# Forgetting attention and an FFN on one core: q and k loaded once for a pair of heads, and one values matmul for the high and low parts of the last 64 by 64 block

## The chip, the core and the metric

The kernel runs on one core of a Trainium2 chip. The core has TensorE for matmuls (PE in the profile; its weight loads, which overlap with the matmuls, have a row of their own, PEld), VectorE (DVE), ScalarE (ACT), GpSimd (POOL) and SyncE (SP), whose queue issues all DMAs of this kernel. They run side by side and wait for one another through semaphores. The metric is the device time of one execution in microseconds, lower is better.

## What is computed

For 8 batches of 8 heads, 576 positions and 64 features a head, causal attention with a decay that is the difference of running sums of log f; the result, 4608 tokens by 512 features, goes through a two-layer FFN with a leaky ReLU.

```python
scores = scale * np.matmul(q, k.transpose(0, 1, 3, 2))
cum = np.cumsum(np.log(np.clip(f, 0.0001, 1.0)), axis=-1)
decay = cum[:, :, :, None] - cum[:, :, None, :]
scores = np.where(causal, -1000000000.0, scores + decay)
scores = scores - np.max(scores, axis=-1, keepdims=True)
attn = np.exp(scores)
attn = attn / (np.sum(attn, axis=-1, keepdims=True) + 1e-09)
x = np.matmul(attn, v)            # heads side by side: (4608, 512)
h = x @ w_in                      # (4608, 2048)
out = np.maximum(0.01 * h, h) @ w_out
```

## The kernel before

All products are made from operands that are rounded to a shorter format (fp32r) for one pass through TensorE. So each operand is kept as a high part and a low part (the rest), and a product is two or three matmuls: high by high, high by low, low by high.

**The FFN** is cut into 18 groups of 256 tokens. `ffn()` yields after each small piece of work (a quantum: 12 matmuls into `h`, or 6 into the sums `o`), and `fill(step)` puts so many quanta between the steps of the attention, so that TensorE always has something to do. Between the layers ACT makes `g`, DVE its rounded part `gh` (L551), and GpSimd the rest `gl` (L553).

**The attention** treats the first 256 positions of three batches ahead of the rest (`early_...`). Then comes one task for each of the 64 heads: `t` 0 to 7 are batch 0, positions 256 to 575; 8 to 47 are five batches with all positions; 48 to 63 are the last two batches, positions from 256 on again. The main loop works on two heads at once: in loop `t`, `scores(t, i)` makes five blocks of rows of head `t`, `transposes(t - 1, i)` and `values(t - 1)` finish head `t - 1`, `load(t + 1)` stands at the top of the loop, and `split(t + 1)` near its end.

- `load` (L223) brings q and k of one head twice, into the lower and the upper 64 partitions of `qraw` and `kraw` (64 features are only half of the partitions); for an even head also v of a pair (`fixed_vm`, L227 and L228).
- `split` (L337 to L347): ACT rounds q to `s1` and k to `m1` on all 128 partitions; a DMA copies the upper half of `s1` to `fixed_s2` (L339); two small DMAs bring decay rows (L340, L341); GpSimd takes the differences into `s1` and `fixed_m2` (L133, the helper `minus`); ACT and GpSimd make the high and low half of the columns of `fixed_vs`, the weights of the values matmuls.
- `scores` (L362 to L376): two matmuls a block, `m1` by `s1` and `m2` by `s2`; DVE adds the mask `tri` and takes the row extreme (L367); ACT takes the exponential (L373) and leaves the block in `fixed_z0` to `fixed_z4`. Block `z4` is 128 rows by 576 columns; its last 64 columns belong to the ragged end of the sequence, and the 64 columns behind them are zero from the start.
- `transposes` (L412): the blocks go through TensorE into a PSUM buffer named `tr`; ACT copies the rounded part to `ph` (L424), DVE the rest to `pl` (L426). `tr_t_1`, the step with i = 1, takes the lower half of the diagonal blocks, and in it the end of `z4`.
- `values` (L451): for each of 4 to 5 column blocks one matmul from `ph` and one from `pl`, all into one PSUM buffer `av` with the weights `fixed_vs`. For the last block, of 64 columns, both have only 64 of 128 partitions that are not zero. ACT and DVE add the two halves of the result to `x` (L458, L459), which frees the buffer.
- `inverse` (L469 to L482) after each second head: the reciprocal sums go to DRAM and come back spread over partitions as `rb` and `rbr`; `normalise` multiplies `x` with them and writes it out, and `xs<-xd` later loads it as an FFN group.

`av`, `tr` and `rt` (of `inverse`) share two PSUM buffers that take turns: each use waits until the one before the last has been read out. Each engine runs its instructions in the order of its list. That order comes from a scheduler with times of its own, not only from the order of the code.

Of the kernel before, what the change touches and what calls it, by code (L numbers as in the profile page):

```python
# [8 lines left out]
F32 = mybir.dt.float32  # L9
# [4 lines left out]
ALU = mybir.AluOpType  # L14

P = 128
# [21 lines left out]
def forgetting_attention_ffn(ctx, tc, qT, kT, v4, vr, f, w_in, w_out, out):  # L38
# [175 lines left out]

    def load(t):

        s, c0, c1 = tasks[t]
        h = state[t] = {}
        a, n = c0 * P, S
        for name, src, lo in (("q", qT, a), ("k", kT, 0)):  # L220
            x = h[name] = one.tile([P, S], F32, tag=f"{name}raw", name=f"{name}raw_{t}")
            for o in range(2):
                nc.sync.dma_start(x[o * D:(o + 1) * D, lo:n], src[s][:, lo:n])  # L223
        if s % 2 == 0:
            g = s // 2
            vm = fixed["vm"]
            nc.sync.dma_start(vm[:, :, :NFULL], v4[g])  # L227
            nc.sync.dma_start(vm[:REST, :, NFULL], vr[g])  # L228
            pairs[s // 2, c0] = {}
# [97 lines left out]
    def split(t):  # L327
# [4 lines left out]
        a, n = c0 * P, S  # L332
        x = "ab"[t % 2]
        s1 = h["s1"] = one.tile([P, S], F32R, tag="s1", name=f"s1_{t}", bufs=2)
        m1 = h["m1"] = one.tile([P, S], F32R, tag="m1", name=f"m1_{t}", bufs=2)
        s2, m2 = h["s2"], h["m2"] = fixed["s2" + x], fixed["m2" + x]
        nc.scalar.copy(s1[:, a:n], h["q"][:, a:n])  # L337
        nc.scalar.copy(m1[:, :n], h["k"][:, :n])
        nc.sync.dma_start(s2[D:, a:n].bitcast(F32), s1[D:, a:n].bitcast(F32))  # L339
        nc.sync.dma_start(s2[2:4, a:n].bitcast(F32), dec_q[s][:, a:n])  # L340
        nc.sync.dma_start(m2[:2, :n].bitcast(F32), dec_k[s][:, :n])  # L341
        minus(s1[:D, a:n], h["q"][:D, a:n], s1[:D, a:n].bitcast(F32))
        minus(m2[D:, :n], h["k"][D:, :n], m1[D:, :n].bitcast(F32))
        o = s % 2
        vs, vm = fixed["vs"][:, o], fixed["vm"][:, o]
        nc.scalar.copy(vs[:, :, :D], vm)
        minus(vs[:, :, D:], vm, vs[:, :, :D].bitcast(F32))  # L347

    def scores(t, i):
# [9 lines left out]
        for x, (a, b) in enumerate(parts):  # L359
# [6 lines left out]
            at = TRI - P + m - n + a  # L366
# [9 lines left out]
        )  # L376

# [10 lines left out]
    def transposes(t, i):  # L388
# [6 lines left out]
        todo, runs, at = [], [], pieces(t, i)[0][3]  # L395
        for x, j, q, skip, m in pieces(t, i):
            todo.append((at - skip, x, j))
            to = place_p(j, q)
            last = runs[-1] if runs else None
            if last and last[4] == 1 and last[1] + last[2] == to:  # L400
                last[2] += m
            elif last and last[2] == m and last[4] > 1 and last[4] * last[3] + last[1] == to:
                last[4] += 1
            elif last and last[2] == m and last[4] == 1 and to > last[1]:
                last[3], last[4] = to - last[1], 2
            else:
                runs.append([at, to, m, 0, 1])
            at += m
# [6 lines left out]
        for dst, eng in ((h["ph"], "a"), (h["pl"], "v")):  # L415
            for a, to, m, step, n in runs:
                if n == 1:
                    o, hi, src = dst[:, to:to + m], h["ph"][:, to:to + m], ps[:, a:a + m]
                else:
                    o = strided(dst, to, n, step, m)  # L420
                    hi = strided(h["ph"], to, n, step, m)
                    src = ps[:, a:a + n * m].rearrange("p (j m) -> p j m", m=m)
                if eng == "a":
                    nc.scalar.copy(o, src)  # L424
                else:
                    nc.vector.tensor_tensor(o, src, hi.bitcast(F32), op=ALU.subtract)  # L426

    def strided(t, start, n, step, m):
        a = t[:, start:start + m]
        return bass.AP(tensor=a.tensor, offset=a.offset, ap=[a.ap[0], [step, n], [1, m]])  # L430
# [208 lines left out]
    for t in range(nt + 1):  # L639
        heads[0] = t < nt  # L640
        if t + 1 < nt:
            load(t + 1)
# [61 lines left out]
```

## Time and profile before

| | |
|---|---|
| three runs | 1220.94 to 1221.28 us, median 1221.16 |
| the profiled execution | 1219.51 us, its span 1217.7 us |
| granted TensorE clock | 0.947 |
| busy: PE, ACT, DVE, POOL | 1193.7, 631.0, 612.8, 429.3 us |
| DMA | 110.54 MB, mean 91 GB/s |
| instructions | 22171 |

The busy time of PE counts each matmul until its last result is out, and matmuls overlap, so it says that PE was seldom empty, not that it ran at its best. What a matmul really takes up is read from the distances between weight loads. In a row of a timeline stand the start in us, the duration in us, engine, line, operation, output<-inputs, the shape (partitions x elements) and in brackets the idle time ahead of it and what ended it. In a row of groups stand the count, the busy sum in us and the mean in ns.

### The profile page before, as it was taken

What the parts mean: (1) busy time and instruction counts of PE and PEld (TensorE: products, weight loads), DVE (VectorE), ACT (ScalarE), POOL (GpSimd) and SP (SyncE); (2) the same over time, 40 slices, a digit from 0 to 9 for tenths busy, and PEclk for the clock granted to TensorE, in tenths of its full rate; (3) what the DMA queues carried; (4) which work ended last, traced back from release to release, by engine and by line L of the source; (5) the groups of instructions that cost most, each with busy time, mean ns of one, the idle gap of its engine ahead of it and who ended that gap; (6) DMA issues with size and microseconds to landing.
All of it is one profiled execution on the core that took longest, in us unless ns stands there. A gap on an engine that the chain in (4) does not pass through costs nothing.

```text
span 1217.7 us, 22171 instructions
## 1 busy us (share of the span) xinstructions
PE 1193.7 (98%) x7876; PEld 1077.6 (88%) x7876; DVE 612.8 (50%) x1682; ACT 631.0 (52%) x1631; POOL 429.3 (35%) x347
## 2 busy tenths in 40 slices
PE   8899999989999999999999999999999999999998
PEld 6678899988889999999999999999999998999997
DVE  7889556656645455544554434344444334553111
ACT  6876456667755565555544545455444444552111
POOL 1000354445444344444434434343344334432000
PEclk9899999989999999999999999999999999999999
DMA  6555234344342233323322223231223122211000
GB/s 208 167 193 171 81 96 119 89 133 112 100 125 80 81 97 107 97 71 96 97 89 60 89 69 95 74 94 54 79 75 92 58 75 75 75 54 46 18 18 19
DMA packets 81103, 110.54 MB, mean 91 GB/s; under 512 B 19616, under 2 KB 50704, under 8 KB 80992
## 3 DMA queue, kind: packets, MB, share of 16 engines
q1 hardware_dynamic: 80992, 109.11, 29.7%
q8 instruction: 63, 1.03, 0.4%
q14 instruction: 48, 0.39, 0.1%
HBM read 82.62 MB, written 18.58 MB: 83 GB/s over the span
## 4 chain that ended last, share of the span: by engine, by line
PE 86%; DMA 5%; DVE 4%; ACT 3%; issue 1%; POOL 0%; SPq 0%; ACTq 0%; DVEq 0%; POOLq 0%
PE h L541 31%; PE o L574 31%; PE av L451 8%; PE tr L412 7%; PE sc L362 7%; DMA xs<-xd 2%; DMA xd<-x 1%; PE sce L256 1%; DVE fixed_z L367 1%; DMA qraw<-in_qT 1%; PE ave L298 1%; DVE pl L426 1%; ACT fixed_z L373 0%; DMA wraw<-in_w_out 0%; DMA wraw<-in_w_in 0%
## 5 line engine op out<-in xcount | busy, mean ns | idle before, releaser
L541 PE MATMUL h<-xh,win_h 128*128 128x256 f32 x1152 | 331.3, 288 | 0.3 <-ACT xh L306 0.3
L541 PE MATMUL h<-xh,win_l 128*128 128x256 f32 x1152 | 327.6, 284 | 0.0
L541 PE MATMUL h<-xs,win_h 128*128 128x256 f32 x1024 | 289.3, 282 | 0.0
L553 POOL TENSOR_TENSOR gl<-g,gh 128x512 fp32r<-128x512 f32 x111 | 143.3, 1291 | 323.9 <-DVE gh L551 315.5
L574 PE MATMUL o<-wout_h,gh 128*128 128x512 f32 x576 | 233.2, 405 | 0.0
L574 PE MATMUL o<-wout_l,gh 128*128 128x512 f32 x576 | 227.0, 394 | 0.0
L574 PE MATMUL o<-wout_h,gl 128*128 128x512 f32 x576 | 225.6, 393 | 0.0
L541 PEld LDWEIGHTS h<-xh,win_h 128*128 128x128 f32 x1152 | 219.9, 191 | 3.5 <-ACT xh L306 0.8
L541 PEld LDWEIGHTS h<-xh,win_l 128*128 128x128 f32 x1152 | 220.3, 191 | 0.8 <-issue 0.7
L373 ACT ACTIVATE fixed_z<-fixed_z,max 128x192 f32<-128x192 f32 (+3 forms) x272 | 161.0, 592 | 105.1 <-DVE max L367 101.2
L367 DVE CUSTOM_DVE_ANT_0 fixed_z<-sc,tri 128x192 f32<-128x192 f32 (+3 forms) x272 | 121.8, 450 | 164.9 <-PE sc L362 162.9
L424 ACT CAST ph<-tr 128x64 fp32r<-128x64 f32 (+3 forms) x360 | 127.0, 374 | 147.2 <-PE tr L412 108.3
L548 ACT ACTIVATE g<-h 128x512 f32<-128x512 f32 x144 | 85.9, 597 | 217.4 <-PE h L541 214.7
L541 PEld LDWEIGHTS h<-xs,win_h 128*128 128x128 f32 x1024 | 195.3, 191 | 2.1
L426 DVE TENSOR_TENSOR pl<-tr,ph 128x64 fp32r<-128x64 f32 (+3 forms) x360 | 145.8, 422 | 76.2 <-ACT ph L424 75.3
L551 DVE CAST gh<-g 128x512 fp32r<-128x512 f32 x144 | 69.0, 479 | 193.9 <-ACT g L548 191.0
L412 PE MATMUL tr<-ident_r,fixed_z 128*128 128x128 f32 x888 | 146.8, 276 | 4.9 <-DVE x L459 2.7
L133 POOL TENSOR_TENSOR s<-qraw,s 64x576 fp32r<-64x576 f32 (+1 forms) x64 | 78.6, 1229 | 190.0 <-ACT s L337 185.3
L412 PEld LDWEIGHTS tr<-ident_r,fixed_z 128*128 128x128 f32 x888 | 109.0, 140 | 24.8 <-DVE x L459 2.9
L574 PEld LDWEIGHTS o<-wout_h,gl 128*128 128x128 f32 x576 | 108.4, 188 | 24.1 <-DVE maxe L269 0.4
L362 PE MATMUL sc<-m,s 128*128 128x288 f32 (+1 forms) x336 | 121.1, 365 | 3.6 <-DVE max L367 3.5
L574 PEld LDWEIGHTS o<-wout_h,gh 128*128 128x128 f32 x576 | 109.0, 189 | 15.7 <-issue 0.4
(107 smaller groups left out, 1687.6 us busy)
## 6 DMA issues: line engine op xcount, KB each, us to landing
kraw<-in_kT SPq DMA_DIRECT2D x128, 144.0 KB
qraw<-in_qT SPq DMA_DIRECT2D x80, 144.0 KB
wraw<-in_w_in SPq DMA_DIRECT2D x16, 512.0 KB
wraw<-in_w_out SPq DMA_DIRECT2D x16, 512.0 KB
fixed_vm<-in_v SPq DMA_DIRECT2D x32, 256.0 KB
xs<-xd SPq DMA_DIRECT2D x16, 512.0 KB
out<-ost SPq DMA_DIRECT2D x28, 256.0 KB
xd<-x SPq DMA_DIRECT2D x20, 288.0 KB
```

Of the source, the lines that this page charges most:

```text
L133: nc.gpsimd.tensor_tensor(out, a, b, op=ALU.subtract)
L362: nc.tensor.matmul(ps[:, :b - a], h["s" + w][:, q:q + P], h["m" + w][:, a:b], start=y == 0, stop=y == 1,)
L367: nc.vector.tensor_tensor_reduce(out=z[:, a:b], in0=ps[:m, :b - a], in1=tri[:m, at:at + b - a], scale=-SCALE, scalar=3.0e38 if x == 0 else ...
L373: nc.scalar.activation(z, z, AF.Exp, bias=h["max"][:m, last:last + 1], scale=-1.0, accum_out=fixed["sum" + "ab"[s // 2 % 2]][:m, i, s % 2: ...
L412: nc.tensor.transpose(ps[:, a:a + P], fixed[f"z{x}"][:, j * P:(j + 1) * P], ident)
L424: nc.scalar.copy(o, src)
L426: nc.vector.tensor_tensor(o, src, hi.bitcast(F32), op=ALU.subtract)
L451: nc.tensor.matmul(ps[:, a - lo:hi - lo], fixed["vs"][:, odd, j, :], h[w][:, at:at + hi - a], start=(n == 0), stop=(n == len(steps) - 1),)
L541: nc.tensor.matmul(ph[:, e, :], w[:, c, fs], xx[:, c, :], start=(c == 0 and x == 0), stop=(c == NCC - 1 and x == 2),)
L548: nc.scalar.activation(g, ph, AF.Prelu, alpha=0.01)
L553: eng.tensor_tensor(gl, g, gh.bitcast(F32), op=ALU.subtract)
L574: nc.tensor.matmul(acc[k], gg[:, e, ts], w[:, e, :], start=(fc_ == 2 * p0 and x == 0), stop=(fc_ == 2 * p1 - 1 and x == 2),)
```

## The change

Three things are changed.

**One load for a pair of heads.** `load` runs only ahead of an even head, at the third step of the loop instead of its top, and puts q and k of the even head into the lower, of the odd head into the upper partitions. What needs a head on the other half is made by copies that move it across partitions: ACT writes one half and DVE, with two new casts a head, the other. The DMA from `s1` to `fixed_s2` is gone. The decay rows keep their own place at the top of the loop (`load_decay`).

**One matmul for the last block.** GpSimd copies the last 64 columns of `z4` into the 64 columns behind them, so that its transpose has the block on both halves of the partitions. ACT's high part is then on both halves, DVE subtracts it in place on the upper half, and GpSimd copies the weights of the block to the upper half as well. One matmul with 128 partitions so adds high and low; the one from `pl` is left out.

**Smaller things.** The mask tile is 128 columns shorter, `rb` and `rbr` are one tile (two DMAs for four), and the row that goes to DRAM lies in a tile with the tag `y`, which `values` uses too.

```diff
     def load(t):
+        for name, src, lo in (("q", qT, a), ("k", kT, 0)):
+            x = raw[name] = one.tile([P, S], F32, tag=f"{name}raw", name=f"{name}raw_{t}")
+            nc.sync.dma_start(x[:, lo:], src[s:s + 2, :, lo:].rearrange("s d n -> (s d) n"))
...
+    def load_decay(t):
...
+        s2, m2 = h["s2"], h["m2"] = fixed["s2" + x], fixed["m2" + x]
+        nc.sync.dma_start(s2[2:4, a:].bitcast(F32), dec_q[s][:, a:])
+        nc.sync.dma_start(m2[:2].bitcast(F32), dec_k[s])
...
     def split(t):
-        nc.scalar.copy(s1[:, a:n], h["q"][:, a:n])
-        nc.scalar.copy(m1[:, :n], h["k"][:, :n])
-        nc.sync.dma_start(s2[D:, a:n].bitcast(F32), s1[D:, a:n].bitcast(F32))
...
-        minus(s1[:D, a:n], h["q"][:D, a:n], s1[:D, a:n].bitcast(F32))
-        minus(m2[D:, :n], h["k"][D:, :n], m1[D:, :n].bitcast(F32))
...
+        mine, other = (low, up) if o == 0 else (up, low)
+        k, q = raw["k"][mine], raw["q"][mine, a:]
+        near, far = (s1[low, a:], s2[up, a:]) if o == 0 else (s2[up, a:], s1[low, a:])
+        nc.scalar.copy(m1[mine], k)
+        nc.vector.tensor_copy(m1[other], k)
+        nc.scalar.copy(near, q)
+        nc.vector.tensor_copy(far, q)
+        minus(m2[up], k, m1[mine].bitcast(F32))
+        minus(s1[up, a:], q, near.bitcast(F32))
...
+        nc.gpsimd.tensor_copy(vs[REST:, NFULL], vs[:REST, NFULL].bitcast(F32))
     def scores(t, i):
...
+        if i == NFULL:
+            z = fixed[f"z{i}"][m - REST:]
+            nc.gpsimd.tensor_copy(z[:, n:], z[:, n - REST:n])
     def transposes(t, i):
...
+        for a, to, m in twice:
+            x = ph[REST:, to:to + m]
+            nc.vector.tensor_tensor(x, ps[REST:, a:a + m], x.bitcast(F32), op=ALU.subtract)
     def values(t, part):
-        steps = [(w, j) for w in ("ph", "pl") for j in range(NCH) if j * P < hi]
+        steps = [("ph", j) for j in range(NCH) if j * P < hi]
+        steps += [("pl", j) for j in range(NFULL) if j * P < hi]
...
         if t + 1 < nt:
-            load(t + 1)
+            load_decay(t + 1)
...
+            if i == 2 and t + 1 < nt and tasks[t + 1][0] % 2 == 0:
+                load(t + 1)
```

On TensorE the list of a head now has one values matmul less; here it is at head 40, first of the kernel before (`ph`, `pl`: high and low part; `o`: sums of the FFN):

```order
L451 MATMUL av_40_0_9143<-pl_40_9023,fixed_vs_1723 128x448 x2
L451 MATMUL av_40_0_9143<-pl_40_9023,fixed_vs_1723 128x320
L451 MATMUL av_40_0_9143<-pl_40_9023,fixed_vs_1723 128x192
L451 MATMUL av_40_0_9143<-pl_40_9023,fixed_vs_1723 128x64
L574 MATMUL o_10_1_0_9157<-wout_h_0_109,gh_10_0_9018 128x512
```

The row of 64 columns is absent in the new list, for each of the 64 heads; otherwise the order of TensorE's work from the first head on is the same but for five places where one FFN matmul changes places with values matmuls.

On GpSimd the list at the first head before (`gl_1_6`: a rest of the FFN; `fixed_m2a` and `s1_2`: the differences of k and q for head 2):

```order
L133 TENSOR_TENSOR s1_2_1929<-qraw_2_1821,s1_2_1929 64x320
L553 TENSOR_TENSOR gl_1_6_1792<-g_1_6_1789,gh_1_6_1791 128x512
L133 TENSOR_TENSOR fixed_m2a_1700<-kraw_2_1824,m1_2_1930 64x576
L133 TENSOR_TENSOR s1_3_2070<-qraw_3_1946,s1_3_2070 64x320
L133 TENSOR_TENSOR fixed_m2b_1708<-kraw_3_1949,m1_3_2071 64x576
```

and now, with the copy of the end of `z4` (L388) of heads 0 and 1:

```order
L583 TENSOR_TENSOR gl_1_6_1788<-g_1_6_1785,gh_1_6_1787 128x512
L133 TENSOR_TENSOR fixed_m2a_1700<-kraw_2_1849,m1_2_1927 64x576
L133 TENSOR_TENSOR s1_2_1926<-qraw_2_1847,s1_2_1926 64x320
L388 COPY fixed_z4_1721<-fixed_z4_1721 64x64
L133 TENSOR_TENSOR fixed_m2b_1708<-kraw_2_1849,m1_3_2062 64x576
L133 TENSOR_TENSOR s1_3_2061<-qraw_2_1847,fixed_s2b_1705 64x320
L388 COPY fixed_z4_1721<-fixed_z4_1721 64x64
```

The copy of a head stands behind the two differences for the head two further on, and the transposes `tr_t_1` of the head wait for it. On DVE the place is the end of a loop; this is head 0 now (the two casts are new; `max` and `fixed_z4` are the row extreme of the last scores block):

```order
L376 ISA fixed_z4_1721,max_0_1762<-sc_0_4_1_1795,tri_176,max_0_1762 128x288
L376 ISA max_0_1762 128x1
L348 CAST m1_2_1927<-kraw_2_1849 64x576
L350 CAST fixed_s2a_1697<-qraw_2_1847 64x320
L428 TENSOR_TENSOR pl_0_1821<-tr_0_1_1822,ph_0_1820 128x64
```

The casts so stand behind the last row extreme of a loop, and from the second loop on ahead of the reciprocal (L469) and of the sums `x<-av` that free the values' PSUM buffers.

More of the change, by code (lines that the diff above doesn't have):

```diff
@@ L393, in transposes @@
         ps = psum.tile([P, 512], F32, tag="tr", name=f"tr_{t}_{i}")
-        todo, runs, at = [], [], pieces(t, i)[0][3]
+        todo, at = [], pieces(t, i)[0][3]
+        runs, low, twice = [], [], []
         for x, j, q, skip, m in pieces(t, i):
             todo.append((at - skip, x, j))
[L398 to L405, printed above, removed]
+            piece = at, place_p(j, q), m
+            add(runs, *piece)
+            if x == j == NFULL:
+                twice.append(piece)
             else:
-                runs.append([at, to, m, 0, 1])
+                add(low, *piece)
             at += m
@@ L414, in transposes, with add, source, strided @@
             )
[L415 to L430, printed above, removed]
+        ph, pl = h["ph"], h["pl"]
+        for run in reversed(runs):
+            nc.scalar.copy(strided(ph, run), source(ps, run))
+        for run in low:
+            nc.vector.tensor_tensor(
+                strided(pl, run), source(ps, run), strided(ph, run).bitcast(F32), op=ALU.subtract
+            )
+        for a, to, m in twice:
+            x = ph[REST:, to:to + m]
+            nc.vector.tensor_tensor(x, ps[REST:, a:a + m], x.bitcast(F32), op=ALU.subtract)
+    def add(runs, at, to, m):
+        last = runs[-1] if runs else None
+        if last and last[4] == 1 and last[1] + last[2] == to and last[0] + last[2] == at:
+            last[2] += m
+        elif last and last[0] + last[2] * last[4] != at:
+            runs.append([at, to, m, 0, 1])
+        elif last and last[2] == m and last[4] > 1 and last[4] * last[3] + last[1] == to:
+            last[4] += 1
+        elif last and last[2] == m and last[4] == 1 and to > last[1]:
+            last[3], last[4] = to - last[1], 2
+        else:
+            runs.append([at, to, m, 0, 1])
+    def source(ps, run):
+        at, to, m, step, n = run
+        x = ps[:, at:at + n * m]
+        return x if n == 1 else x.rearrange("p (j m) -> p j m", m=m)
+    def strided(t, run):
+        at, to, m, step, n = run
+        a = t[:, to:to + m]
+        return a if n == 1 else bass.AP(
+            tensor=a.tensor, offset=a.offset, ap=[a.ap[0], [step, n], [1, m]]
+        )
     def place_p(j, q):
@@ L479, in inverse @@
         a = c0 * P
[L480 to L485 removed]
+        for o in range(2):
+            nc.sync.dma_start(
+                main[o * D:(o + 1) * D, a:], to[o:o + 1, a:].broadcast_to([D, NCH * P - a])
+            )
+        pairs[s // 2, c0]["r"] = main
     def normalise(t):
```

52 lines of the change are left out of this document (21 added, 31 removed).

## The prediction

> **What bounds the kernel now.** I read the busy times first, then the chain that ended last, then PE by stretches of the run, then PE's waits.
>
> ```profile
> PE 1193.7 (98%) x7876; PEld 1077.6 (88%) x7876; DVE 612.8 (50%) x1682; ACT 631.0 (52%) x1631; POOL 429.3 (35%) x347
> ...
> PE 86%; DMA 5%; DVE 4%; ACT 3%; issue 1%; POOL 0%; SPq 0%; ACTq 0%; DVEq 0%; POOLq 0%
> ```
> ```profile
> 0.00:160.00 160.00, 151.02 (x895) 120.80 (x896) 124.04 (x256) 103.05 (x244) 21.72 (x35) 0.94 0.50 163
> 160.00:360.00 200.00, 192.06 (x1294) 175.03 (x1292) 117.67 (x370) 130.83 (x361) 94.52 (x75) 0.94 0.37 108
> 360.00:1125.00 765.00, 761.54 (x5129) 701.20 (x5130) 353.21 (x1027) 384.63 (x1007) 312.88 (x238) 0.95 0.27 80
> ```
> ```profile
> PE tr L412 <- DVE x L459: 2.7, 1, 2.7
> PE tr L412 <- DVE pl L426: 2.2, 4, 0.8
> ```
>
> The second fence gives for each stretch its length and the busy time of PE, PEld, DVE, ACT and POOL (then clock and DMA). From 360 to 1125 us PE is empty for 3.5 of 765 us: there a matmul less is time less, and a step on another engine costs only what it takes beyond its slack. From 160 to 360 us, heads 0 to 16, PE is empty for 8 of 200 us: the loops are short and buffers come free late. So the question has two parts: what one matmul takes up, and which of the new steps reaches PE in these early loops.
>
> **The matmul that goes.** 64 are left out, one a head.
>
> ```profile
> L451 PE MATMUL av<-pl,fixed_vs 128*128 128x64 f32 x64 | 13.8, 215 | 0.0
> ```
> ```profile
> 471.31 0.19 PEld L451 LDWEIGHTS av<-pl,fixed_vs 128*128 128x128 f32 x1
> 471.42 0.19 PEld L574 LDWEIGHTS o<-wout_h,gh 128*128 128x128 f32 x1
> 471.53 0.19 PEld L574 LDWEIGHTS o<-wout_l,gh 128*128 128x128 f32 x1
> 471.77 0.19 PEld L574 LDWEIGHTS o<-wout_h,gl 128*128 128x128 f32 x1
> ```
>
> 215 ns is its way through the array, most of it beside its neighbours, so 64 x 0.215 would be too much. The pace is read from the weight loads: one starts when the matmul ahead of it takes over the weights loaded before. The row at 471.31 loads the weights of the 64-column matmul; the next load starts 0.11 later, and the one after it again 0.11 later, while behind a matmul of 512 columns the distance is 0.24 (471.53 to 471.77). By its columns the small one would need 64/512 x 0.24 = 0.03. It takes 0.11 because the next weights have to come in first: the load is the limit, not the stream. Without it the load of `o<-wout_h,gh` starts at 471.31, and all behind it is 0.11 earlier. **64 x 0.11 = 7.0 us** are saved; the ends are 64 x 0.03 = 1.9 (if the load were hidden) and 13.8, which the overlap excludes.
>
> The skill has a rule for this. The Trainium skill, "TensorE: Matmul & The Clock Gate", section "Back-to-back issue gap", gives some 81 ns a matmul at 128 columns for a stream of loads and matmuls: by it an estimate of 64 x 0.081 = 5.2 us; the trace's 0.11 is larger, and the sum goes by the trace.
>
> **The copy of the end of z4.** The page has no such copy on POOL. From below there is the smallest POOL write, from above the subtractions, which read two inputs:
>
> ```profile
> 148.51 0.14 POOL L322 MEMSET fixed_z<- 128x64 f32 x1
> ```
> ```profile
> L133 POOL TENSOR_TENSOR s<-qraw,s 64x576 fp32r<-64x576 f32 x40 | 57.0, 1426 | 103.6 <-ACT s L337 103.6
> L133 POOL TENSOR_TENSOR s<-qraw,s 64x320 fp32r<-64x320 f32 x24 | 21.6, 899 | 86.5 <-ACT s L337 81.7 <-DMA rbr<-rows 4.7
> ```
>
> 256 columns more cost 0.53, so 64 columns cost 0.90 - 0.53 = 0.37 as a subtraction; with 0.14 below I take 0.3. Its length matters less than its place: it stands behind both subtractions for a later head, and the transposes wait for it. At the first head:
>
> ```profile
> 161.93 0.88 POOL L133 TENSOR_TENSOR s<-qraw,s 64x320 fp32r<-64x320 f32 x1 [3.46 <-ACT s L337]
> 162.76 1.28 POOL L553 TENSOR_TENSOR gl<-g,gh 128x512 fp32r<-128x512 f32 x1
> 164.13 1.44 POOL L133 TENSOR_TENSOR fixed_m2a<-kraw,m 64x576 fp32r<-64x576 f32 x1
> ```
> ```profile
> 161.53 0.43 DVE L551 CAST gh<-g 128x512 fp32r<-128x512 f32 x1
> 161.88 0.51 DVE L367 CUSTOM_DVE_ANT_0 fixed_z<-sc,tri,max 128x288 f32<-128x288 f32 x1
> ```
> ```profile
> 162.45 0.77 ACT L373 ACTIVATE fixed_z<-fixed_z,max 128x576 f32<-128x576 f32 x1
> 163.48 0.38 PE L412 MATMUL tr<-ident_r,fixed_z 128*128 128x128 f32 x2
> ```
>
> PE took up the transposes of `z4` at 163.48, just behind the exponential (162.45 + 0.77 = 163.2). Now POOL first has `gl` (from 161.96, when `gh` is there, to 163.2), the difference of k (1.44, to 164.7), of q (0.88, to 165.6) and the copy (to 165.9), with the two new DVE casts in between (below, up to 0.5). So the transposes start at 165.9 to 166.4, 2.4 to 2.9 us late, and PE's list has nothing that may pass them: **2.7 us given back**, once. At head 11, in the short loops, POOL and PE stood so:
>
> ```profile
> 275.68 1.42 POOL L133 TENSOR_TENSOR s<-qraw,s 64x576 fp32r<-64x576 f32 x1 [5.13 <-ACT s L337]
> 277.18 1.44 POOL L133 TENSOR_TENSOR fixed_m2b<-kraw,m 64x576 fp32r<-64x576 f32 x1
> ```
> ```profile
> 278.98 0.38 PE L412 MATMUL tr<-ident_r,fixed_z 128*128 128x128 f32 x2
> 279.33 0.66 PE L412 MATMUL tr<-ident_r,fixed_z 128*128 128x128 f32 x4
> ```
>
> POOL is through at 278.6, the transposes with `z4` are those at 279.33: 0.7 us for a copy of 0.3. In these loops it just fits or is late by tenths (in the next sum). Late in the run it has room:
>
> ```profile
> 797.72 1.44 POOL L133 TENSOR_TENSOR fixed_m2b<-kraw,m 64x576 fp32r<-64x576 f32 x1
> ...
> 803.33 0.39 PE L412 MATMUL tr<-ident_r,fixed_z 128*128 128x128 f32 x2
> 805.16 0.61 PE L412 MATMUL tr<-ident_r,fixed_z 128*128 128x128 f32 x4
> ```
>
> The four transposes at 805.16 are those with `z4`; POOL was through at 799.16, 6.0 us earlier. There it costs nothing.
>
> **The two casts on DVE.** 512 columns took 0.43 at 161.53; 1024 take 0.69:
>
> ```profile
> 152.98 0.69 DVE L513 CAST xh<-xs 128x1024 fp32r<-128x1024 f32 x1
> ```
>
> so 576 columns need 0.46. What weighs is with whom they share. Here DVE and POOL in the same two microseconds:
>
> ```profile
> 704.40 1.62 DVE L494 TENSOR_TENSOR x<-x,rb 128x512 f32<-128x512 f32 x1
> 705.95 0.89 DVE L494 TENSOR_TENSOR x<-x,rbr 128x64 f32<-128x64 f32 x1
> ```
> ```profile
> 704.18 1.29 POOL L553 TENSOR_TENSOR gl<-g,gh 128x512 fp32r<-128x512 f32 x1 [2.01 <-DVE gh L551]
> 705.43 1.32 POOL L133 TENSOR_TENSOR fixed_vs<-fixed_vm,fixed_vs 128x320 fp32r<-128x320 f32 x1
> ```
>
> DVE's first row ends 0.55 behind the end of `gl` (705.47), and its second, of only 64 columns, ends with POOL's next (706.75): the two take turns, one instruction each. So a cast that meets the subtractions waits for one, and the second cast for the next.
>
> The Trainium skill, "SBUF — State Buffer", section "SBUF: two separate sides", has the rule: such DVE instructions and POOL share a port pair under an exclusive lock, and the loser blocks for a whole instruction. It speaks against this change, and the rows agree with it; if they ran freely side by side, the next sum would be 0.
>
> Who waits behind the casts? The additions to `x`, which free PSUM buffers. In a short loop:
>
> ```profile
> 277.52 0.62 DVE L459 TENSOR_TENSOR x<-av,y 64x448 f32<-64x448 f32 x1
> 278.46 0.28 DVE L459 TENSOR_TENSOR x<-av,y 64x128 f32<-64x128 f32 x1 [0.33 <-ACT y L458]
> ```
>
> The second addition ends at 278.74, and PE takes its buffer for the transposes at 279.33: 0.6 of slack. Now the subtraction of k comes first and runs to about 277.1, the second cast waits for it and ends near 277.4. In each second loop the reciprocal stands next on DVE and has to take its turn as well, either against the copy (0.3) or against the subtraction of q (1.4). The additions then come 0.5 or 1.6 later than at 277.52, which costs the loop nothing or 1.0 us. There are eight such loops up to head 15; in the others no reciprocal stands there. From below 0 (all fit), from above 8 x 1.0 = 8; near the row I take about 0.15 for each, **1.1 us with the tenths of the copies**. Late, the addition at
>
> ```profile
> 798.15 0.62 DVE L459 TENSOR_TENSOR x<-av,y 64x448 f32<-64x448 f32 x1 [0.22 <-ACT y L458]
> ```
>
> has until 803.33, 4.5 us, and two turns of 1.44 with two casts are 3.5: nothing.
>
> **Loads, and the rest.** The DMAs lose the doubled q and k and the copy between tiles; the load for an even head moves from the top of the loop to its third step, but on SP's list it still stands right behind the decay rows, and it waited for POOL's subtractions there before, too. What ACT waited for q and k,
>
> ```profile
> ACT m L338 <- DMA kraw<-in_kT: 5.7, 5, 2.3
> ```
>
> can only shrink; PE is not released by it, so I take 0, with 2 us of gain as the other end. GpSimd's copy of weights stands behind the one of `fixed_vs`, a loop ahead of its use; the row in the tile `y` is read by its DMA long before `values` writes there. All that at 0; if that cover went, each would be a wait for 0.3 to 2 us in 32 or 64 loops.
>
> **The sum.** -7.0 + 2.7 + 1.1 = -3.2 us. The profiled execution took 1219.51 us, so it would take 1216.3; the runs' median is 1.65 higher, and on its scale I predict **1218.0**.
>
> **The rivals.** (a) As worked out: 1216.5 to 1219.5, chance 0.54. (b) The copy finds POOL free (`gl` or the loads come at another time): 1221.16 - 7.0 = 1214.2; for it: all slack behind 360 us; against it: the list at the first head; 0.15. (c) The turns cost more in the early loops, 0.6 to 0.9 in each of eight, and the gain is all but gone: 1219.5 to 1222; for it: slacks of 0.6; 0.20. (d) Slower: where `gl` stands ahead of both subtractions and the second cast comes behind three turns, the additions are 1.3 + 1.43 + 1.44 + 0.6 = 4.8 late, more than the 4.5 of slack in the late loops. It decides from 4.5; at 0.3 over it in some 48 loops it gives back 14 us more, 1232. Against it: the casts stand ahead of that, and POOL is 35% busy; 0.05. (e) The matmul that goes was worth only its columns, 1.9 us: 1221.16 - 1.9 + 3.8 = 1223.1; against it are the weight loads; 0.06.
>
> **How the numbers follow.** About 0.2% (2.4 us) is what a measurement of this kernel can tell from no change, so the line lies at 1218.7. Faster: three quarters of (a) and all of (b), 0.56; slower: (d) and a little of (e), 0.06; the rest, 0.38, is within 0.2%. The range is 1214.0 to 1222.0: (a), (c) and nearly all of (b); outside are (d), (e) and the case that loads bring 2 us on top.
>
> **What would show it.** PE has 64 matmuls less (7812), the load behind the values starts 0.11 earlier in each head, and PE's busy share from 360 us on stays at 99%. POOL's copy at the first head ends at 165.9 or later with PE empty for 2 to 3 us ahead of `tr`. DVE's casts show 0.46 alone and 1 to 2 us beside a subtraction, and PE's waits for `x` and `pl` grow by about a microsecond in all, ahead of 360 us. It is wrong if PE waits for DVE or POOL in late loops, or if the first transposes come on time.

## The result, and the profile after

The changed kernel takes 1228.38 us (median of 5 runs, 1225.41 to 1231.2); the kernel before takes 1220.94 us in 5 runs beside it. The ratio is 1.0073 (95% interval 1.0048 to 1.0098): it is slower by 0.7%. The profiled execution took 1228.38 us, its span is 1226.6 us, 8.9 us longer than that of before.

From the page of the changed kernel: the busy times, and the chain of work that ended last.

```profile
PE 1197.8 (98%) x7812; PEld 1074.2 (88%) x7812; DVE 756.7 (62%) x1810; ACT 632.5 (52%) x1631; POOL 483.6 (39%) x475
...
PE 81%; DVE 7%; DMA 4%; ACT 3%; POOL 2%; issue 2%; SPq 0%; POOLq 0%; ACTq 0%; DVEq 0%
```

PE has its 64 matmuls less (7812) and is nevertheless busy for 4.1 us more: a part of its matmuls ran slowly. DVE's busy time has grown by 143.9 us, for 128 instructions more (the two casts): 1.1 us each, where one that meets nothing on POOL takes 0.46. In the chain DVE's share goes from 4% to 7%, POOL's from 0 to 2%.

The same three stretches as before (length, then busy time of PE, PEld, DVE, ACT and POOL, then clock, DMA share, GB/s):

```profile
0.00:160.00 160.00, 152.76 (x887) 120.25 (x888) 123.97 (x256) 102.71 (x243) 23.18 (x37) 0.99 0.50 160
160.00:360.00 200.00, 188.09 (x1217) 168.91 (x1216) 151.47 (x392) 127.91 (x347) 103.77 (x105) 0.97 0.22 69
360.00:1125.00 765.00, 759.00 (x5092) 696.27 (x5091) 460.47 (x1127) 388.20 (x1019) 354.26 (x333) 1.00 0.19 59
```

From 160 to 360 us PE gets through 1217 matmuls where it did 1294, and is empty for 11.9 us in place of 7.9; behind 360 us it is empty for 6.0 in place of 3.5. The DMAs' share of these 200 us fell from 0.37 to 0.22; no row here shows a gain from that.

Where the time went is seen best by pairing the matmuls of the two traces: the n-th transposition of a pair's reciprocals (tile `rt`, one for two heads) of one run with the n-th of the other. The table gives how much later it starts in the changed kernel (the first row: the matmul `h` there; the times are those of the kernel before, from the first instruction of the trace).

| at (before, us) | 140 | 172.6 | 231.3 | 355.2 | 387.5 | 446.9 | 478.7 | 577.0 | 613.5 | 912.3 | 944.1 | 1100.3 |
|---|---|---|---|---|---|---|---|---|---|---|---|---|
| later by (us) | 1.1 | 5.4 | 5.3 | 11.4 | 10.4 | 10.0 | 12.4 | 11.7 | 12.5 | 10.2 | 10.6 | 9.0 |

Four things stand in it: a step of 4.3 us at the first head; a climb of 5 us in the short loops up to 387 us; slopes downward, where the missing matmuls pay (2.3 us for the 16 heads from 613.5 to 912.3, 0.14 each); and steps of 2.4, 0.8 and 0.4 us late, which the prediction had at nothing. A large part of the climb is a slower clock and not waiting. Between 231.3 and 387.5 us of the kernel before, and between the same instructions of the changed kernel, PE's emptiness is 7.7 and 8.8 us, but the time at half clock is 3.4 and 10.2 us. At half clock about half the work is done (22 matmuls in the 6.8 us from 260.2 us, 44 in the 6.8 us behind them), so of the 5.1 us up to 3.4 are the 6.8 us more at half clock. This stretch of the changed kernel holds two of these half clocks (6.8 us from 260.2, 3.4 from 355.8; the clock stands ahead of the DMA share, and 1.00 is full):

```profile
260.00:360.00 100.00, 93.85 (x596) 83.80 (x597) 73.82 (x203) 65.23 (x182) 49.70 (x49) 0.95 0.24 75
```

**The first head.** POOL, DVE and PE of the changed kernel (start, duration, engine and line, and in brackets what ended the idle time ahead of it):

```profile
163.15 1.29 POOL L583 TENSOR_TENSOR gl<-g,gh 128x512 fp32r<-128x512 f32 x1 [2.87 <-DVE gh L581]
164.52 1.49 POOL L133 TENSOR_TENSOR fixed_m2a<-kraw,m 64x576 fp32r<-64x576 f32 x1
165.97 0.93 POOL L133 TENSOR_TENSOR s<-qraw,s 64x320 fp32r<-64x320 f32 x1
166.96 0.24 POOL L388 COPY fixed_z<-fixed_z 64x64 f32<-64x64 f32 x1
```
```profile
163.53 1.22 DVE L348 CAST m<-kraw 64x576 fp32r<-64x576 f32 x1
164.68 1.51 DVE L350 CAST fixed_s2a<-qraw 64x320 fp32r<-64x320 f32 x1
```
```profile
167.25 0.44 PE L421 MATMUL tr<-ident_r,fixed_z 128*128 128x128 f32 x2 [2.52 <-POOL fixed_z L388]
```

POOL's list is the predicted one, `gl`, two subtractions, then the copy, and PE stands empty for 2.52 us. What comes behind it was not foreseen. Stretches around the wait; the figure behind POOL's is the granted clock:

```profile
164.34:168.00 3.66, 1.14 (x7) 0.61 (x5) 1.85 (x2) 0.34 (x3) 2.72 (x4) 1.00 0.01 2
168.00:171.50 3.50, 3.50 (x16) 3.37 (x15) 2.01 (x8) 1.53 (x6) 0.00 (x0) 0.51 0.00 0
171.50:175.00 3.50, 3.50 (x28) 3.37 (x27) 2.02 (x7) 2.46 (x6) 0.65 (x1) 1.00 0.02 4
```

For 3.4 us the clock is half: 16 matmuls in 3.5 us, 28 in the next. PE counts as busy all that time, which is where its added busy time comes from. Wait and half clock together are the 4.3 us.

**The short loops.** One with the reciprocal in it, about 310 us: DVE, POOL, PE.

```profile
307.12 1.21 DVE L350 CAST s<-qraw 64x576 fp32r<-64x576 f32 x1
308.37 1.28 DVE L499 TENSOR_SCALAR r<-fixed_suma 128x10 f32<-128x10 f32 x1
...
309.82 0.56 DVE L489 TENSOR_TENSOR x<-av,y 64x448 f32<-64x448 f32 x1
310.76 0.28 DVE L489 TENSOR_TENSOR x<-av,y 64x128 f32<-64x128 f32 x1 [0.38 <-ACT y L488]
```
```profile
306.57 1.45 POOL L133 TENSOR_TENSOR fixed_m2b<-kraw,m 64x576 fp32r<-64x576 f32 x1 [4.21 <-ACT m L347]
307.98 1.64 POOL L133 TENSOR_TENSOR s<-qraw,fixed_s2b 64x576 fp32r<-64x576 f32 x1
309.56 0.24 POOL L388 COPY fixed_z<-fixed_z 64x64 f32<-64x64 f32 x1
```
```profile
310.43 0.44 PE L421 MATMUL tr<-ident_r,fixed_z 128*128 128x128 f32 x2 [0.18 <-DVE x L489]
311.19 0.63 PE L421 MATMUL tr<-ident_r,fixed_z 128*128 128x128 f32 x4 [0.18 <-DVE x L489]
```

The cast of q ends (308.33) when POOL's first subtraction has (308.02) and DVE has had its turn; the reciprocal's addition of 10 columns takes 1.28 and ends (309.65) with the second subtraction (309.62). So the first addition to `x` ends at 310.38, and PE's transposes start at 310.43: the slack of 0.6 is used up, and PE waits 0.18 us here and 0.18 again at 311.19. Each further tenth reaches PE. The cast of k isn't in these rows, because in DVE's list of this loop it stands ahead of the last row extreme (305.48, 0.46 us) and not behind it as at the first head. That is so in 13 of the 64 loops; in 11 of them the cast takes 0.45 or 0.46 us.

**Late.** Where the step of 2.4 us lies: DVE from the casts to the cast of the next group, POOL's subtraction for the next values' weights, SP's issues, and then the same addition, issues and cast of the kernel before.

```profile
464.93 1.23 DVE L348 CAST m<-kraw 64x576 fp32r<-64x576 f32 x1
466.08 1.68 DVE L350 CAST fixed_s2a<-qraw 64x576 fp32r<-64x576 f32 x1
467.80 0.63 DVE L489 TENSOR_TENSOR x<-av,y 64x448 f32<-64x448 f32 x1
...
469.13 1.50 DVE L522 TENSOR_TENSOR x<-x,rb 128x512 f32<-128x512 f32 x2
...
478.09 0.69 DVE L543 CAST xh<-xs 128x1024 fp32r<-128x1024 f32 x1 [4.59 <-DMA xs<-xd]
```
```profile
469.39 1.17 POOL L133 TENSOR_TENSOR fixed_vs<-fixed_vm,fixed_vs 128x320 fp32r<-128x320 f32 x1 [1.52 <-issue]
```
```profile
470.58 0.58 SPq L225 DMA_DIRECT2D fixed_vm<-in_v  x1
471.26 0.56 SPq L527 DMA_DIRECT2D xd<-x  x1
...
474.70 0.39 SPq L538 DMA_DIRECT2D xs<-xd  x1
```
```profile
456.37 0.63 DVE L459 TENSOR_TENSOR x<-av,y 64x448 f32<-64x448 f32 x1 [1.49 <-ACT y L458]
...
465.99 0.69 DVE L513 CAST xh<-xs 128x1024 fp32r<-128x1024 f32 x1 [0.89 <-DMA xs<-xd]
```
```profile
459.24 0.35 SPq L497 DMA_DIRECT2D xd<-x  x1
459.69 0.57 SPq L227 DMA_DIRECT2D fixed_vm<-in_v  x1
...
461.68 0.54 SPq L508 DMA_DIRECT2D xs<-xd  x1
```

Before, the first addition stood at 456.37 after 1.49 us of idleness; 10 us later it would be 466.4. It comes at 467.80, right behind two casts that took 1.23 and 1.68. The normalisation (469.13 to 470.63) is late with it, by 1.4 us counted from the `rt` transposition ahead of it. A second delay comes from SP's list. Before, the write of `x` stood ahead of the load of the next values and was issued at 459.24, as soon as the normalisation was through (459.22). Now the load stands ahead of it and is issued when POOL's subtraction that reads the old values ends (470.56). So the write goes out at 471.26, 0.63 us behind the normalisation, and the read of the next group (`xs`) 3.44 us behind the write in place of 2.44: 1.6 us more, of which 0.9 comes back because the cast `xh` starts 3.39 behind the read's issue in place of 4.31. Together `xh` is 2.1 us late. DVE now sits idle for it for 4.59 us in place of 0.89, with the subtractions of `pl` and the additions to `x` behind it in its list. PE has no 2 us of slack there and is empty for 1.45 us. At the step of 0.8 us (613.5) the load stood ahead of the write before, too; there the normalisation alone is 1.0 us late.

### The profile page after: what moved, and what is told of

It is laid out like the page before. It is cut to its first block, busy times and chain, and to the rows that moved or that the text cites. A ratio compares the mean times of both kernels' runs of the same rounds, so it can differ in the third digit from the quotient of the medians.

```text
span 1226.6 us, 21745 instructions
## 1 busy us (share of the span) xinstructions
PE 1197.8 (98%) x7812; PEld 1074.2 (88%) x7812; DVE 756.7 (62%) x1810; ACT 632.5 (52%) x1631; POOL 483.6 (39%) x475
## 4 chain that ended last, share of the span: by engine, by line
PE 81%; DVE 7%; DMA 4%; ACT 3%; POOL 2%; issue 2%; SPq 0%; POOLq 0%; ACTq 0%; DVEq 0%
PE o L604 29%; PE h L571 28%; PE tr L421 7%; PE av L481 6%; PE sc L371 6%; DMA xs<-xd 2%; DMA xd<-x 2%; DVE fixed_z L376 1%; PE sce L263 1%; DVE pl L428 1%; ACT fixed_z L382 1%; PE ave L305 1%; DVE m L348 1%; DVE wraw L169 1%; DVE wraw L165 1%
## 5 line engine op out<-in xcount | busy, mean ns | idle before, releaser
L426 ACT CAST ph<-tr 128x192 fp32r<-128x192 f32 (+3 forms) x360 | 126.4, 373 | 142.4 <-PE tr L421 109.4
L428 DVE TENSOR_TENSOR pl<-tr,ph 128x384 fp32r<-128x384 f32 (+3 forms) x296 | 137.7, 468 | 72.9 <-ACT ph L426 72.1
L604 PEld LDWEIGHTS o<-wout_l,gh 128*128 128x128 f32 x576 | 109.0, 189 | 14.6
```

What stands on the lines that cost most here:

```text
L426: nc.scalar.copy(strided(ph, run), source(ps, run))
L428: nc.vector.tensor_tensor(strided(pl, run), source(ps, run), strided(ph, run).bitcast(F32), op=ALU.subtract)
L604: nc.tensor.matmul(acc[k], gg[:, e, ts], w[:, e, :], start=(fc_ == 2 * p0 and x == 0), stop=(fc_ == 2 * p1 - 1 and x == 2),)
```

## The experiments

The experiments were timed in four groups (1 to 4, 5 to 8, 9 and 10, 11 and 12), each on one chip beside the kernel before, which had medians from 1219.2 to 1220.3 us there. Differences below are taken from the kernel before of the same group; a median compared with one of another group carries up to a microsecond from that. Where two traces are compared, one execution of each is.

| kernel | median us | before | difference | ratio (95% interval) |
|---|---|---|---|---|
| the change | 1228.4 | 1220.9 | +7.4 | 1.0073 (1.0048 to 1.0098) |
| shared matmul alone | 1215.5 | 1219.2 | -3.7 | 0.9970 (0.9955 to 0.9986) |
| loads for a pair alone | 1229.7 | 1219.2 | +10.5 | 1.0085 (1.0065 to 1.0105) |
| change, z4's copy on ACT | 1225.3 | 1219.2 | +6.2 | 1.0050 (1.0032 to 1.0069) |
| change, casts on ACT | 1217.6 | 1219.2 | -1.6 | 0.9987 (0.9971 to 1.0004) |
| change, casts and copy on ACT | 1223.1 | 1220.3 | +2.8 | 1.0019 (0.9996 to 1.0041) |
| shared matmul, z4's copy on ACT | 1212.0 | 1220.3 | -8.3 | 0.9921 (0.9899 to 0.9943) |
| change, cast of q on ACT | 1222.0 | 1220.3 | +1.7 | 1.0011 (0.9995 to 1.0028) |
| change, subtractions on DVE | 1220.7 | 1220.3 | +0.4 | 0.9993 (0.9976 to 1.0011) |
| before, 64 matmuls left out | 1211.5 | 1219.6 | -8.2 | 0.9927 (0.9907 to 0.9947) |
| change, the wait filled | 1228.8 | 1219.6 | +9.2 | 1.0075 (1.0050 to 1.0101) |
| shared matmul, copy on ACT, two more ACT copies | 1219.8 | 1219.2 | +0.6 | 1.0014 (0.9994 to 1.0033) |
| the same, two more DVE copies | 1230.4 | 1219.2 | +11.2 | 1.0089 (1.0061 to 1.0118) |

**1. The shared matmul alone.** The functions `transposes`, `add`, `source`, `strided` and `values` of the change, with the two copies on POOL:

```
+        nc.gpsimd.tensor_copy(vs[REST:, NFULL], vs[:REST, NFULL].bitcast(F32))
...
+        if i == NFULL:
+            z = fixed[f"z{i}"][m - REST:]
+            nc.gpsimd.tensor_copy(z[:, n:], z[:, n - REST:n])
```

> The kernel before with the shared values matmul alone (loads, splits and normalisation as before). Theory A (read from the two traces: the 64 matmuls are worth 0.11 us each, 7.0 in all; the copy of the end of z4 costs the first head 2.9 us of waiting and about 1.4 more because TensorE runs at half clock behind the wait; everything else of the loss comes from the loads): 1220.9 - 7.0 + 4.3 = 1218.2 us. Rival B (the copy also costs in each short loop up to 360 us): 1221 or more. Rival C (the order of the first 150 us moves with any edit and gives 1 us either way): 1217 to 1219. PE should stand empty about 2.5 us ahead of the first transposes of z4.

1215.5 us, 3.7 less than before. The wait at the first head is there (PE empty for 2.11 us, a half clock of 3.4 us behind it). So this half of the change is a gain. Theory A's sum is 2.7 us above it; 1.7 of that is the kernel before, which took 1219.2 us here and not the 1220.9 that the sum starts from.

**2. The loads for a pair alone.** The change with `transposes`, `values` and z4 as before.

> The kernel before with the loads for a pair of heads alone (two casts on DVE, loads at the third step of the loop, one tile for the reciprocal's rows), high and low parts in two values matmuls as before. Theory A (the loss sits in the loads: some 5 us in the short loops up to 360 us, some 3 in late stalls, 1 in the start): 1220.9 + 9 = 1230 us. Theory as predicted blind (casts cost 1.1 us in all): 1222. If the loads are free and the loss belongs to the merging: 1221 or less.

1229.7 us, 10.5 more than before: theory A by its time, and the whole loss, and more, lies in this half. Paired with the trace of before, it is 4.3 us later at the first head already; it climbs by 2.6 us from 231.3 to 387.5 us, where its time at half clock is the same 3.4 us, and it has the late steps: 2.6 us at 478.7 and 1.0 at 613.5.

**3. The copy of z4 on ACT.**

```
-            nc.gpsimd.tensor_copy(z[:, n:], z[:, n - REST:n])
+            nc.scalar.copy(z[:, n:], z[:, n - REST:n])
```

> The changed kernel with the copy of the end of z4 on ACT, right behind the exponential, in place of POOL. Theory A: the wait of 2.5 us at the first head and the half clock behind it go: 1228.4 - 4.3 = 1224.1 us, and the clock's stretch at 168 us is gone from the profile. Rival B (POOL has the copy behind its subtractions in the short loops too): 1222 or less. Rival D (ACT is as late, 64 copies of 0.25 to 0.35 us on its path): 1228 or more.

1225.3 us: 3.1 less than the change by the medians, 1.2 by the differences from before, and the intervals overlap; theory A had 4.3. The trace is sharper: the wait ahead of the first transposes is 0.59 us, there is no half clock behind it, and PE is 3.7 us earlier at 170 us than in the changed kernel (0.2 of it from the start). The copy's place at the first head is confirmed, as a smaller part of the loss.

**4. The casts on ACT.** One thing is moved and nothing of the loads:

```
-        nc.vector.tensor_copy(m1[other], k)
+        nc.scalar.copy(m1[other], k)
...
-        nc.vector.tensor_copy(far, q)
+        nc.scalar.copy(far, q)
```

> The changed kernel with the two casts of k and q that it puts on DVE done on ACT instead; loads and their places as in the change. Theory A (DVE casts take turns with POOL's subtractions, and what stands behind them on DVE frees PE's buffers late): the 8 us of the short loops and of the late stalls go, 1220 us. Rival E (the loss comes from where the loads stand on SP's list): stays at 1228. Rival F (ACT, with 1.1 us more in each head, takes DVE's place as the engine that is late in the short loops): 1226 to 1232.

1217.6 us: 9 to 11 us go with the two casts, so the loss as a whole doesn't come from the place of the loads on SP's list (rival E). The paired traces show where it goes. Of 13.3 us between the changed kernel's execution and this one, 3.8 lie ahead of 158 us, where the traces of the runs scatter by several microseconds; 2.6 go at the first head (no half clock behind a wait of 1.53 us), 6.4 up to 387.5 us (up to 3.4 of them half clock, which lasts 3.4 us there in place of 10.2), and only 0.5 behind that. So theory A's late stalls did not go with the casts: the steps are still there, 1.7 us at 478.7 and 0.7 at 613.5. In this run, too, SP's list has the load of the next values ahead of the write (0.62 us behind the normalisation, the read 3.40 behind the write). What the casts did to POOL is seen in its groups, first of the changed kernel, then of this one (mean ns behind the busy time):

```profile
L133 POOL TENSOR_TENSOR fixed_m2b<-kraw,m 64x576 fp32r<-64x576 f32 x32 | 50.4, 1576 | 65.4 <-ACT m L347 64.3 <-PE h L571 0.2
...
L133 POOL TENSOR_TENSOR s<-qraw,s 64x576 fp32r<-64x576 f32 x20 | 32.8, 1641 | 0.0
```
```profile
L133 POOL TENSOR_TENSOR fixed_m2b<-kraw,m 64x576 fp32r<-64x576 f32 x32 | 46.8, 1464 | 62.2 <-ACT m L347 60.9
...
L133 POOL TENSOR_TENSOR s<-qraw,s 64x576 fp32r<-64x576 f32 x20 | 29.5, 1474 | 0.4 <-ACT s L349 0.4
```

Without the casts beside them the subtractions take 0.11 to 0.17 us less; both sides pay for the turns.

**5. Casts and copy on ACT.** Edits 3 and 4 together.

> The changed kernel with both corrections: the two casts of k and q and the copy of the end of z4 on ACT. If the two parts add (the copy 3.1 us and the casts 10.8 us, as measured one by one): 1228.4 - 13.9 = 1214.5 us. Rival: with the casts gone POOL is earlier and the copy no longer late, so that the copy on ACT gives nothing more: 1217.6. Rival: ACT, with four casts and the copy, becomes the late engine in the short loops: 1219 or more.

1223.1 us: the two gains do not add. Of the three answers the third (ACT late) is nearest, and run 11 below agrees with it; but its profiled execution also had 13.7 us of half clock in the first 60 us, where run 4 had 3.4, and the intervals of 4 and 5 touch. Over its 12 executions, too, the mean granted clock is lower, 0.9935 against 0.997 (medians), which alone makes some 4 of the 5.5 us. How much of the difference between them is ACT stays open.

**6. The shared matmul with the copy on ACT.** Run 1 with edit 3.

> The kernel before with the shared values matmul and the copy of the end of z4 on ACT; loads as before. If the 64 matmuls are worth 7.0 us and the copy on POOL was what kept the run with the shared matmul alone at 3.7: 1219.2 - 7.0 = 1212 us. Rival (the copy on ACT costs what it saves on POOL): 1215.5.

1212.0 us, 8.3 less than before, ratio 0.9921 (0.9899 to 0.9943): faster than both kernels. PE waits 0.41 us at the first head.

**7. Only the cast of q on ACT.** The second line of edit 4.

> The changed kernel with only the cast of q on ACT; the cast of k stays on DVE. If the price is that of turns with POOL (the cast of k took 0.90 us on average and that of q 1.1 to 1.6 in place of 0.45): the second cast, which meets the second subtraction, carries more than half: 1220 to 1222 us. Rival (the price is 0.45 us of DVE time each, or any delay of DVE's list, turns or not): the two are equal and half of 10.8 us goes, 1223. Rival (one cast is enough to make DVE late): 1226 or more.

1222.0 us, at the edge of what the theory of turns said; 1223, the rival, lies within the spread too. By the medians the cast of q carries 6.4 of the 10.8 us and that of k, which comes first, 4.4 (by the differences from before, 5.7 and 3.3); this leans to turns but does not tell them from plain DVE time.

**8. The subtractions on DVE.**

```
-        minus(m2[up], k, m1[mine].bitcast(F32))
-        minus(s1[up, a:], q, near.bitcast(F32))
+        nc.vector.tensor_tensor(m2[up], k, m1[mine].bitcast(F32), op=ALU.subtract)
+        nc.vector.tensor_tensor(s1[up, a:], q, near.bitcast(F32), op=ALU.subtract)
```

> The changed kernel with the subtractions for the low parts of k and q on DVE in place of POOL, behind the two casts. Theory of turns: DVE has four instructions of about 0.45, 0.45, 0.7 and 0.7 = 2.3 us a head that meet nothing of POOL but gl and the values' subtraction, where two casts beside POOL took 0.9 + 1.4 = 2.3 us before: DVE's busy time stays near 757 us (744 to 790), though it does 128 instructions more, the copy of z4 is not late, and the time is 1224 to 1229. Rival (DVE and POOL don't hinder one another; it is DVE's own work that is too much): DVE's busy time rises by 80 us or more and the time to 1235 or more.

DVE has 128 instructions more than in the changed kernel and is busy for 15 us less (the page's line):

```profile
PE 1194.4 (98%) x7812; PEld 1072.4 (88%) x7812; DVE 741.5 (61%) x1938; ACT 633.1 (52%) x1631; POOL 313.3 (26%) x347
```

That tells turns from plain work: the two casts take 58.9 us in all here and took 143.8 in the changed kernel, so more than half of what DVE spent on them was waiting for POOL. The time, 1220.7 us, is even 3 us below the theory's: POOL, 170 us less busy, is early, so that the first head's transposes wait only 0.17 us for the copy, and the late steps at 478.7 and 613.5 us are gone. There POOL is through with the old values 1.0 us before the normalisation ends, and the load ahead of the write no longer holds it up (0.33 us in place of 0.63).

**9. The price of the matmuls.** The kernel before, without the 64 matmuls of the last block's low part.

```
+        steps = [x for x in steps if x != ("pl", NFULL)]
```

> The kernel before with the 64 values matmuls of the last block's low part left out and nothing put in their place (so the low part of that block is missing in the sums; everything else is as before): the price of the matmuls by themselves. By 0.11 us each: 1220.3 - 7.0 = 1213 us. By their columns alone (0.03 us): 1218.4. If their whole way through the array counted (0.215): 1206.5.

1211.5 us: 8.2 less (6.5 to 11.3 by the interval), 0.13 each. Neither the columns alone (1.9 in all) nor the whole way through the array (13.8). Run 6, which computes everything, is as fast as this one: sharing gets the whole price.

**10. The wait filled.** Ahead of the first head's transposes:

```
+            if t == 1 and i == 1:
+                busy = psum.tile([P, 512], F32, tag="h", name="busy")
+                for _ in range(24):
+                    nc.tensor.matmul(busy[:, :P], ident_r, ident_r, start=True, stop=True)
```

> The changed kernel with 24 matmuls of 128 columns that compute nothing needed, ahead of the first head's transposes, where TensorE stood empty for 2.5 us waiting for the copy on POOL. If the half clock behind that wait (3.41 us at 0.5 from 168.1 us) comes from the emptiness: the transposes start as late as in the changed kernel, but no half clock follows, and TensorE is some 1.4 us earlier from 175 us on; by the time, 1227. Rival (the half clock comes in any case there): the stretch at 168 us is seen again, 1228.4 or more.

PE of this kernel, then its stretches with the granted clock behind POOL's figure:

```profile
166.66 2.79 PE L684 MATMUL busy<-ident_r 128*128 128x128 f32 x24
170.27 0.44 PE L421 MATMUL tr<-ident_r,fixed_z 128*128 128x128 f32 x2 [0.82 <-POOL fixed_z L388]
```
```profile
167.00:170.50 3.50, 2.68 (x25) 2.54 (x24) 2.19 (x2) 0.39 (x2) 3.07 (x4) 1.00 0.01 2
170.50:174.00 3.50, 3.50 (x24) 3.14 (x23) 1.69 (x6) 1.56 (x6) 0.00 (x0) 1.00 0.00 0
```

The transposes still wait for the copy, as late as in the changed kernel (this execution was 3.0 us later from the start on); the half clock is gone. Emptiness was its cause. PE gains 0.6 us there and not 1.4, because the building of the program moved four matmuls `o` (0.23 each) from ahead of the transposes to behind them. The time, 1228.8 us of 4 runs, can't show so little.

**11 and 12. More copies in the fastest kernel.** To run 6, whose loads are those of before, two copies a head are added, once on ACT and once on DVE (here the latter):

```
         nc.scalar.copy(m1[:, :n], h["k"][:, :n])
+        nc.vector.tensor_copy(m1[:D, :n], h["k"][:D, :n])
+        nc.vector.tensor_copy(m1[:D, a:n], h["k"][:D, a:n])
```

> The kernel before with the shared values matmul and the copy of z4 on ACT (1212.0 us, loads as before), with two more ACT copies a head of the size of the two casts (k's first rows written again to the same place; nothing else waits for them). What is open: with the pair's loads and the casts on ACT this took 1223.1 us, 11 more. If ACT's 1.1 us more a head are the cause: 1219 to 1223. If it is the way the pair's loads stand (order of the loads, splits and subtractions): 1212 to 1214.

> The same kernel of 1212.0 us with the two more copies a head on DVE, behind ACT's cast of k, beside POOL's subtractions; loads, DMAs and the rest as before. If the price of the change lies in two DVE copies that take turns with POOL, wherever the loads stand: 0.9 and 1.1 to 1.6 us each in place of 0.45, DVE's busy time up by about 100 to 140 us, and the time up by 8 to 12 us: 1220 to 1224. If the copies are harmless without the pair's loads: 1212 to 1214.

1219.8 us with ACT, 8 to 9 more than run 6; 1230.4 with DVE, 18 to 20 more. From the DVE kernel, its groups of added copies and its stretch of short loops, and then the same stretch of run 6:

```profile
L340 DVE CAST m<-kraw 64x576 fp32r<-64x576 f32 x40 | 62.9, 1571 | 1.3
...
L339 DVE CAST m<-kraw 64x576 fp32r<-64x576 f32 x64 | 55.6, 868 | 7.3 <-ACT m L338 4.6 <-issue 2.1
```
```profile
220.00:340.00 120.00, 106.57 (x664) 93.67 (x663) 87.36 (x220) 73.25 (x207) 54.62 (x48) 0.94 0.34 100
340.00:1120.00 780.00, 773.26 (x5196) 709.47 (x5195) 474.16 (x1175) 413.69 (x1110) 348.42 (x296) 1.00 0.28 82
```
```profile
220.00:340.00 120.00, 113.82 (x760) 102.69 (x759) 75.48 (x235) 83.23 (x240) 59.80 (x54) 0.99 0.40 114
340.00:1120.00 780.00, 775.82 (x5211) 712.47 (x5210) 372.32 (x1054) 405.28 (x1081) 336.56 (x290) 1.00 0.29 81
```

The copies take 0.87 and 1.57 us as in the change, wherever the loads stand, and 96 matmuls fewer fit into the 120 us of short loops; behind 340 us the two differ by 15 of some 5,200. DVE's busy time is 132.6 us above run 6, as expected. The price is more than the 8 to 12 expected: three half clocks more follow PE's waits (0.94 in that stretch; up to 5 us), and these copies also wait for ACT's cast (4.6 us in all). So two copies a head beside POOL's subtractions make a loss of this size without the pair's loads. For ACT the price is less sure: 8 to 9 us here, but run 4, with the pair's loads and two casts more on ACT, is only 2.1 above run 1.

That the pair's loads cost nothing does not follow. Between the `rt` transpositions at 387.5 and 1100.3 us of the table, the runs without half clock there (all but run 5) take: 712.8 (before) and 715.5 (run 2) with all matmuls; without the 64, 707.3 to 708.2 (runs 1, 6, 9 and 11) with the loads as before, and 710.8 to 712.5 (the change, runs 3, 4, 7 and 10) with the pair's loads, whether the casts are on DVE or on ACT. Run 12, with the loads as before and DVE's copies, takes 709.2; run 8, where POOL is early, 707.1. So the change (711.4) loses 4.0 us late against run 6 (707.4), and run 4, whose casts are on ACT, still loses 3.5. The row that shows how is the load ahead of the write of `x`. No run moves that load alone, so its share is read from the traces.

## Why the prediction was wrong

It said 1218.0 us, 3 below before; it became 7.4 above, outside its range at the upper end.

- **What bounds the kernel:** right. The two stretches, short loops and full PE, are where each part acted. The half clock behind a wait is not in it.
- **The matmul, -7.0:** right. Left out alone it is worth 8.2 us (run 9), and 7.0 lies within the interval. Rival (e), 1.9 us, is out. By the Trainium skill, "TensorE: Matmul & The Clock Gate", section "Back-to-back issue gap", the estimate would have been 5.2 us, below the run's interval.
- **The copy of z4, +2.7 at the first head:** place, list and wait were right (2.52 us of emptiness; the copy ended at 167.2 where 165.9 or later was written). The size was not: 4.3 us, because the wait brings a half clock behind it.
- **The casts, +1.1: the step that failed.** The mechanism, one turn for each instruction, was right, and so was the 0.46 for a cast alone. What was wrong is "about 0.15 for each" of eight loops: 1.1 us stood for what measured 5. The groups of the changed kernel:

```profile
L348 DVE CAST m<-kraw 64x576 fp32r<-64x576 f32 x64 | 57.3, 896 | 2.1
...
L350 DVE CAST s<-qraw 64x576 fp32r<-64x576 f32 x20 | 31.8, 1588 | 0.1
L350 DVE CAST fixed_s2a<-qraw 64x576 fp32r<-64x576 f32 x20 | 28.8, 1438 | 0.2
```

  By the trace only 9 of the 64 casts of k overlap nothing on POOL, and none of the 64 of q. The prediction had assumed that the casts fit into gaps in most loops and lose tenths in the others; they meet a subtraction nearly always, and the second meets the next. The term is 5 us net in the short loops (from 5.3 to 10.4 in the table), more with what the missing matmuls gave back there. Up to 3.4 of the 5 are the half clocks, which the prediction did not have at all; in the traces of runs 2 and 3, with the casts on DVE and no more half clock than before, the same stretch is 2.6 and 2.2 us longer. The bounds of 0 to 8 held all that; the value was taken at the wrong end, from the slack of one loop, without adding up DVE's list for every kind of loop.
- **Late: nothing, the second error.** The additions had their 4.5 us of slack, as written, and rival (d) did not come about. But the normalisation is in the same list, and its end starts a row of transfers (write of `x`, read of `xs`, cast of the next group) that had not been followed: steps of 2.4 and 0.8 us. An engine's delay was priced only through the PSUM buffers it frees, not through the DMAs that it starts. Run 12 against run 6, both with the loads of before, has steps of 0.8 and 0.9 us at these places: turns are enough for the second and for a third of the first. The third step, of 0.4 us, is not the change's delays: runs 1, 6 and 9 have 0.3 to 0.6 us there against before.
- **Loads, 0:** too low. The transfers saved bought nothing, and most of the price lies in the two copies that replace them (runs 4, 8 and 12). But the prediction followed only where the loads of q and k stand on SP's list. The load of v now stands ahead of the write of `x`, which it delays at 471.26 us; late in the run the kernels with the pair's loads lose about 3.5 us, with the casts on ACT too (run 4).
- **What is left:** 1.1 us by 140 us. Of the changed instructions only a few stand ahead of it, for heads 0 and 1. The order of PE's list differs there, and the half clocks at the start fall differently from execution to execution; at that place the traces of the other runs lie from 3.1 us earlier to 6.6 us later than before. It was not tried apart.

The sum by the table: 1.1 + 4.3 + 5.0 up to 387 us, and from there -5.0 for the matmuls and +3.6 for the three steps, 9.0 at 1100 us.

## What to carry to other kernels

A copy moved onto DVE beside GpSimd's work cost a turn here and not its own duration: 0.9 to 1.6 us on average for 0.46. Follow DVE's list to everything behind it, the stores and the next loads included, and do the same with the list of the DMA queue: a load that moves can come to stand ahead of a store. The transfers saved here were off the critical path and bought nothing. And where TensorE is full, price a wait of two microseconds with the half clock behind it, which cost 1.7 us more at the first head.

## What the runs showed that was not expected

- **The half clock.** It came behind gaps of 2.52 us (the first head) and even of 1.24 us, with 0.32 more soon after (run 4, at 250 us), here:

```profile
251.58 0.44 PE L421 MATMUL tr<-ident_r,fixed_z 128*128 128x128 f32 x2 [1.24 <-DVE x L489]
```
```profile
252.80:256.20 3.40, 3.40 (x13) 2.76 (x11) 1.32 (x6) 1.42 (x7) 2.39 (x3) 0.51 0.33 88
```

  but not behind the 1.97 us at 343 us of the kernel before. Each lasts 3.41 us or twice that, and within one execution they start at multiples of 3.413 from one another (17.9, 168.1, 260.2 and 355.8 us in the changed kernel). So the traces can be cut into these periods, and then what counts is how long PE is empty within one of them. From 150 us on, over all 14 traces and leaving out the periods that are at half clock themselves: in 19 periods PE was empty for 1.86 us or more, and all 19 are followed by half clock; in 10 it was from 1.43 to 1.82, and 4 of them are; with 1.39 or less none is. The 1.97 us at 343 us are cut by the grid into 1.35 and 0.62. The Trainium skill, "TensorE: Matmul & The Clock Gate", section "HAM oscillation — how this bites in real kernels", warns of gaps over some 3.4 us; in these runs 1.9 us within one period were enough.
- **The spread between executions** goes with it: of the kernel before's 29 executions beside runs 5 to 8, those with a mean granted clock of 0.997 or 0.998 took 1217.4 to 1220.0 us, those at 0.990 or below 1223.6 to 1226.9.
- **A clock recorded as 0.95** in the profile of before, against 1.00 in that of the change, made no difference to the pace: in the last stretch, where nothing waits, the distance between the two runs stays at 8.88 us from 1120 us to the end.
